# A conv and Fourier-mix kernel on one core: 128-row tiles without overlap, an engine order written by hand, and a second stage on 64-row tiles

## The chip, the core and the metric

The kernel runs on one core of a Trainium2 chip. Its five engines are called as in the profile: PE (matmul, with PEld for the loads of the stationary operand), DVE, ACT, POOL and SP. PE, DVE and ACT reach PSUM; SP and POOL issue the DMAs. The metric is device time in microseconds (us). Three runs of the kernel before gave 261.29, 263.11 and 265.54 us, a median of 263.11 us.

## What is computed

The input x is (8, 3264, 192) in float32: 8 batches, 3264 positions (rows), 192 channels. The first half is a causal convolution of 7 taps along the positions, with one softmax-normalised set of taps for each of 8 heads of 24 channels. The second half is a Fourier layer on the result c: the lowest 64 modes along the positions are mixed by complex 192x192 matrices (`w_r`, `w_i`, one pair a mode), transformed back and added, and a dense layer with a clamp at zero is added on top.

```python
c = conv7_causal(x, softmax(weight))         # per head, along S
X = rfft(c, axis=1)[:, :64]
Yr = Xr @ w_r - Xi @ w_i                     # per mode
Yi = Xr @ w_i + Xi @ w_r
u = c + irfft(Y, n=3264)
out = u + maximum(u @ w_ch, 0)
```

## The kernel before

The positions of a batch are cut into 27 windows of 122 rows. A window is loaded as 128 rows, the 6 rows before it included (`load_win`, L58 to L61), so that one banded 128x128 matrix per head (`cband`) makes 122 rows of convolution in one matmul (`conv_unit`, L214). The loads cast to bf16 on their way into `x_all`; POOL issues them, 3 units of 8 to 10 windows a batch. The convolution's PSUM result goes back into `x_all` by ACT (L226).

`dft` (L268) multiplies each window with a table of cosines and sines (`fst`, made at L143 to L156) and adds 27 windows up into 64 modes for one batch; `xtrans` (L278) turns that round and DVE writes it to `xt` (L286). The mixing loop (L315) then takes 4 modes a turn: 12 matmuls on 32-column tiles of PE (L321) against the mode matrices, which POOL loads through a ring of 6 tiles of 2 modes (L198 to L205). In the same loop the convolved windows are turned by PE into `cT` (`t_unit`, L257, transposes at L264, copies by DVE at L266), since the last stage needs channels on the partitions, and the table is turned into `gst` (`g_part`, L304). The order of the instructions on each engine is made by a scheduler from dependencies and program order; it moves transposes forward into the convolution.

The last stage makes pairs of windows of two batches (`group`, L376). `zp` collects (c + irfft) @ w_ch: one matmul of 384 columns with the table `gst` (L382) and four of 192 columns with `cT` (L386, L387) per window; `yp` gets irfft alone (L388). `zwi`, made by `zwi_pair` (L359), holds the mixed modes multiplied by w_ch and by one. ACT clamps `zp` into `r` (L392), DVE adds `x_all` to `yp` into `t` (L401), and a second add puts `r` on top (L404), on POOL for two groups in three and on DVE for the third. A tile `t` holds 4 windows; `store` (L406) sends it out by SP in 4 DMAs, rows 0 to 111 and rows 112 to 121 of each batch apart. There are 54 groups, three buffers of `t`, and two buffers each of `zp` and `yp`, which fill PSUM.

Of the kernel before, what the change touches and what calls it, by code (L numbers as in the profile page):

```python
# [13 lines left out]
BF16 = mybir.dt.bfloat16  # L14
PSUM = bass.MemoryType.PSUM
# [3 lines left out]
def kernel(  # L19
# [16 lines left out]
    P = 128  # L36
    WIN = 122
    OV = KK - 1
    NWIN = 27
    LASTVALID = S - WIN * (NWIN - 1)  # L40
    PAIRS = NWIN // 2
    NSLOT = 3 * PAIRS + 2
    CTW = NSLOT * WIN + 6
    GW = NWIN * WIN + 6
    MG = 2
    NGRP = MODES // MG
    TWOPI = 2.0 * math.pi
    MAGIC = 12582912.0
    UNITS = ((0, 10), (10, 8), (18, 9))
    USLOTS = ((0, 15), (15, 12), (27, 14))  # L50

    constp = ctx.enter_context(tc.tile_pool(name="const", bufs=1))

    x_all = constp.tile([P, B, NWIN, D], BF16, tag="x_all")

    def load_win(b, c0, n):  # L58
        off = (b * S + WIN * c0 - OV) * D
        src = bass.AP(tensor=x.tensor, offset=x.offset + off, ap=[[D, P], [WIN * D, n], [1, D]])  # L60
        nc.gpsimd.dma_start(out=x_all[:, b, c0:c0 + n, :], in_=src)  # L61

    def load_unit(b, u):
        w0, n = UNITS[u]
        if b == 0 and u == 0:
            nc.gpsimd.dma_start(out=x_all[OV:OV + 112, 0, 0, :], in_=x[0, 0:112, :])
            nc.gpsimd.dma_start(out=x_all[OV + 112:P, 0, 0, :], in_=x[0, 112:WIN, :])
            load_win(0, 1, n - 1)
        elif b == B - 1 and u == 2:
            load_win(b, w0, n - 1)  # L70
# [18 lines left out]

    earlyp = tc.tile_pool(name="early", bufs=1, side="right")
    early_stack = ExitStack()
    ep = early_stack.enter_context(earlyp)
    cband = ep.tile([P, H, P], BF16, tag="cband")
    fst = ep.tile([P, NWIN, 2 * MODES], BF16, tag="fst")
    xt = ep.tile([P, 3, MODES + 1, 2 * B], BF16, tag="xt")

    with tc.tile_pool(name="setup", bufs=1) as sp:
        wraw = sp.tile([P, H, KK], F32, tag="wraw")  # L100
        nc.sync.dma_start(out=wraw[:], in_=bass.AP(tensor=weight.tensor, offset=weight.offset,
                                                   ap=[[0, P], [KK, H], [1, KK]]))
        ones_b = sp.tile([P, P], BF16, tag="ones_b")
        nc.vector.memset(ones_b[:], 1.0)
        maskk = sp.tile([P, KK, P], BF16, tag="maskk")
        for k in range(KK):
            nc.gpsimd.affine_select(out=maskk[:, k, :], in_=ones_b[:], compare_op=ALU.is_equal, fill=0.0,
                                    base=-k, pattern=[[-1, P]], channel_multiplier=1)
        wmax = sp.tile([P, H], F32, tag="wmax")
        nc.vector.reduce_max(out=wmax[:], in_=wraw[:], axis=AX.X)  # L110
        wsub = sp.tile([P, H, KK], F32, tag="wsub")
        nc.vector.tensor_tensor(out=wsub[:], in0=wraw[:],
                                in1=wmax[:, :].unsqueeze(2).to_broadcast([P, H, KK]), op=ALU.subtract)
        wexp = sp.tile([P, H, KK], F32, tag="wexp")
        nc.scalar.activation(out=wexp[:], in_=wsub[:], func=ACT.Exp)
        wsum = sp.tile([P, H], F32, tag="wsum")
        nc.vector.reduce_sum(out=wsum[:], in_=wexp[:], axis=AX.X)
        nc.vector.tensor_scalar(out=wsum[:], in0=wsum[:], scalar1=1e-9, scalar2=None, op0=ALU.add)
        wrec = sp.tile([P, H], F32, tag="wrec")
        nc.vector.reciprocal(out=wrec[:], in_=wsum[:])  # L120
        wsb = sp.tile([P, H, KK], F32, tag="wsb")
        nc.vector.tensor_tensor(out=wsb[:], in0=wexp[:],
                                in1=wrec[:, :].unsqueeze(2).to_broadcast([P, H, KK]), op=ALU.mult)
        for h in range(H):
            nc.vector.tensor_scalar(out=cband[:, h, :], in0=maskk[:, 0, :], scalar1=wsb[:, h, 0:1],
                                    scalar2=None, op0=ALU.mult)
            for k in range(1, KK):
                nc.vector.scalar_tensor_tensor(out=cband[:, h, :], in0=maskk[:, k, :],  # L128
                                               scalar=wsb[:, h, k:k + 1], in1=cband[:, h, :],
                                               op0=ALU.mult, op1=ALU.add)  # L130

        sidx = sp.tile([P, NWIN], F32, tag="sidx")
        nc.gpsimd.iota(sidx[:], pattern=[[WIN, NWIN]], base=0, channel_multiplier=1,
                       allow_small_or_imprecise_dtypes=True)
        midx = sp.tile([P, MODES], F32, tag="midx")
        nc.gpsimd.iota(midx[:], pattern=[[1, MODES]], base=0, channel_multiplier=0,
                       allow_small_or_imprecise_dtypes=True)
        halfpi = sp.tile([P, 1], F32, tag="halfpi")
        nc.vector.memset(halfpi[:], math.pi / 2)  # L140
        kprod = sp.tile([P, NWIN, MODES], F32, tag="kprod")
        turns = sp.tile([P, NWIN, MODES], F32, tag="turns")
        nc.vector.tensor_tensor(out=kprod[:],  # L143
                                in0=sidx[:, :].unsqueeze(2).to_broadcast([P, NWIN, MODES]),
                                in1=midx[:, :].unsqueeze(1).to_broadcast([P, NWIN, MODES]),
                                op=ALU.mult)
        nc.vector.tensor_scalar(out=turns[:], in0=kprod[:], scalar1=1.0 / S, scalar2=MAGIC,
                                op0=ALU.mult, op1=ALU.add)
        nc.vector.tensor_scalar(out=turns[:], in0=turns[:], scalar1=-MAGIC, scalar2=float(S),
                                op0=ALU.add, op1=ALU.mult)  # L150
        nc.vector.tensor_tensor(out=kprod[:], in0=kprod[:], in1=turns[:], op=ALU.subtract)
        nc.vector.tensor_scalar(out=kprod[:], in0=kprod[:], scalar1=-float(S) / 2, scalar2=float(S) / 2,
                                op0=ALU.max, op1=ALU.min)
        nc.scalar.activation(out=fst[:, :, MODES:2 * MODES], in_=kprod[:], func=ACT.Sin, scale=-TWOPI / S)
        nc.scalar.activation(out=turns[:], in_=kprod[:], func=ACT.Abs)
        nc.scalar.activation(out=fst[:, :, 0:MODES], in_=turns[:], func=ACT.Sin, scale=-TWOPI / S,  # L156
                             bias=halfpi[:, 0:1])

    load_unit(0, 2)
    for b in range(1, B):  # L160
        for u in range(3):
            load_unit(b, u)

# [5 lines left out]
    ascale = constp.tile([P, 1], F32, tag="ascale")  # L170
    nc.vector.memset(ascale[:], 2.0 / S)
    nc.vector.memset(ascale[0:1, :], 1.0 / S)
    nc.vector.memset(ascale[64:65, :], 1.0 / S)

    win0 = constp.tile([P, 2 * D], BF16, tag="win0")
    win1 = constp.tile([P, 2 * D], BF16, tag="win1")
    wB0 = constp.tile([P, D], BF16, tag="wB0")
    nc.gpsimd.memset(win0[:, D:2 * D], 0.0)
    nc.gpsimd.memset(win1[:], 0.0)  # L180
# [277 lines left out]
```

## Time and profile before

| what | value |
|---|---|
| runs | 261.29, 263.11, 265.54 us (median 263.11) |
| profiled execution, span from first to last instruction | 264.2 us |
| busy: PE, PEld | 172.3 us (65%), 130.4 us (49%) |
| busy: DVE, ACT, POOL | 154.7 us (59%), 105.9 us (40%), 138.7 us (52%) |
| HBM read, written | 40.31 MB, 20.05 MB |
| mean granted TensorE clock | 0.883 of full speed |

The span counts instructions alone; the page gives no other time of the profiled execution, and the span lies within the three runs. "Busy" is the sum of an engine's instructions; waiting instructions are not in it. The page's slices are 40 equal parts of the span, 6.6 us each. The chain that ended last is followed back from the last instruction, each step to what released it. The trace's GB/s counts the bytes that the DMA engines write, so a cast load of 4-byte numbers into 2-byte ones counts half of what it reads.

### The profile page before, as it was taken

How to read it: one execution, taken by the hardware profiler on the slowest of the kernel's cores; microseconds unless marked ns; L12 is line 12 of the kernel's file. 1: busy time of each engine (PE TensorE's matmuls, PEld its weight loads, DVE VectorE, ACT ScalarE, POOL GpSimd, SP SyncE). 2: the span in 40 equal slices, each digit the busy share in tenths (PEclk: the TensorE clock that was granted, in tenths of full speed). 3: DMA queues.
4: the chain of work that ended last, by engine and by line, in shares of the span. 5: the costliest groups of instructions: out<-in, count | busy, mean ns of one | idle time of the engine just before them, and what ended most of it. 6: DMA issues, size and time to landing. Idle time of an engine off the chain costs nothing.

```text
span 264.2 us, 4507 instructions
## 1 busy us (share of the span) xinstructions
PE 172.3 (65%) x1699; PEld 130.4 (49%) x1699; DVE 154.7 (59%) x264; ACT 105.9 (40%) x140; POOL 138.7 (52%) x154
## 2 busy tenths in 40 slices
PE   0137405508999985978873479887886868877800
PEld 0015204507989973756641157665564547655500
DVE  3997121013344376699971128877865787788730
ACT  2027709205799732211112126453444344445410
POOL 8944435534500017657664016775758497578740
PEclk9999855755999999799996559999999999999965
DMA  5999999999930009999999104876596667877692
GB/s 54 168 192 192 192 192 192 192 192 116 162 59 2 0 2 132 196 175 147 160 169 168 25 0 107 221 204 196 155 258 179 187 169 220 240 219 193 189 254 63
DMA packets 65341, 40.51 MB, mean 153 GB/s; under 512 B 31016, under 2 KB 65320, under 8 KB 65320
## 3 DMA queue, kind: packets, MB, share of 16 engines
q0 software_dynamic: 37600, 20.14, 58.1%
q1 hardware_dynamic: 27720, 20.09, 27.7%
q8 instruction: 13, 0.21, 0.3%
q14 instruction: 8, 0.07, 0.1%
HBM read 40.31 MB, written 20.05 MB: 228 GB/s over the span
## 4 chain that ended last, share of the span: by engine, by line
PE 36%; DMA 27%; DVE 14%; POOL 12%; ACT 4%; issue 3%; SPq 1%; DVEq 0%; POOLq 0%; ACTq 0%
DMA x_all<-in_x_dram 18%; POOL t L404 7%; PE xp L272 7%; DVE t L401 6%; PE cp L220 5%; PE tp L264 5%; DMA wt<-in_moe_w_i_dram 5%; PE zp L382 4%; DMA out_dram<-t 4%; PE zp L386 4%; PE zp L387 4%; DVE cT L266 3%; PE yp L388 3%; ACT r L392 3%; PE yp L321 2%
## 5 line engine op out<-in xcount | busy, mean ns | idle before, releaser
L404 POOL TENSOR_TENSOR t<-t,r 122x768 f32<-122x768 f32 x36 | 69.2, 1944 | 43.2 <-DVE t L401 32.4
L392 ACT ACTIVATE r<-zp 122x768 f32<-122x768 f32 (+1 forms) x54 | 43.1, 809 | 51.3 <-POOL t L404 36.1
L401 DVE TENSOR_TENSOR t<-yp,x_all 122x768 f32<-122x768 f32 (+1 forms) x54 | 50.0, 951 | 21.3 <-PE yp L388 14.6
L226 ACT CAST x_all<-cp 122x960 bf16<-122x960 f32 (+2 forms) x48 | 39.6, 884 | 31.9 <-PE cp L220 21.1
L382 PE MATMUL zp<-zwi,gst 128*128 128x384 bf16 x108 | 35.9, 332 | 18.2 <-ACT r L392 15.4
L386 PE MATMUL zp<-win,cT 128*128 128x192 bf16 x216 | 46.0, 250 | 0.0
L220 PE MATMUL cp<-x_all,cband 128*128 128x240 bf16 (+2 forms) x192 | 31.0, 297 | 20.4 <-DVE cband L128 16.4
L203 POOL DMA_DIRECT2D wt<-in_moe_w_r_dram x32 | 19.5, 611 | 44.2 <-PE yp L321 36.7
L386 PEld LDWEIGHTS <-cT 128*128 128x128 bf16 x216 | 21.4, 99 | 25.6 <-issue 23.8
L220 PEld LDWEIGHTS <-cband 128*128 128x128 bf16 x192 | 20.3, 111 | 26.3 <-DVE cband L128 17.6
L61 POOL DMA_DIRECT2D x_all<-in_x_dram x24 | 23.5, 993 | 18.5 <-DMA x_all<-in_x_dram 18.5
L266 DVE COPY cT<-tp 128x854 bf16<-128x854 bf16 (+2 forms) x48 | 28.4, 609 | 4.2 <-PE tp L264 3.7
L264 PE MATMUL tp<-ident,tl 122*128 122x122 bf16 x112 | 22.1, 228 | 11.1 <-DVE tl L233 10.9
L264 PE MATMUL tp<-ident,x_all 122*128 122x122 bf16 x216 | 26.4, 228 | 3.4 <-DVE cT L266 2.6
L404 DVE TENSOR_TENSOR t<-t,r 122x768 f32<-122x768 f32 (+1 forms) x18 | 25.7, 1430 | 3.3 <-ACT r L392 2.6
L388 PE MATMUL yp<-zwi,gst 128*128 128x384 bf16 x108 | 26.3, 331 | 1.2 <-DVE t L401 1.2
L272 PE MATMUL xp<-x_all,fst 122*128 122x192 bf16 (+1 forms) x216 | 25.4, 265 | 0.8 <-ACT fst L156 0.8
L387 PEld LDWEIGHTS <-cT 128*128 128x128 bf16 x216 | 21.4, 99 | 8.3 <-issue 0.7
L387 PE MATMUL zp<-win,cT 128*128 128x192 bf16 x112 | 24.0, 249 | 0.0
L387 PE MATMUL zp<-wB,cT 128*128 128x192 bf16 x104 | 22.3, 250 | 0.0
L264 PEld LDWEIGHTS <-x_all 122*128 122x128 bf16 x216 | 18.4, 103 | 7.2 <-issue 5.5
L272 PEld LDWEIGHTS <-fst 122*128 122x128 bf16 (+1 forms) x216 | 20.3, 106 | 2.3 <-ACT fst L156 1.2
(83 smaller groups left out, 189.5 us busy)
## 6 DMA issues: line engine op xcount, KB each, us to landing
out_dram<-t SPq DMA_DIRECT2D x48, 336.0 KB
wt<-in_moe_w_r_dram POOLq DMA_DIRECT2D x32, 144.0 KB, 5.0
wt<-in_moe_w_i_dram POOLq DMA_DIRECT2D x32, 144.0 KB, 5.0
x_all<-in_x_dram POOLq DMA_DIRECT2D x8, 432.0 KB, 17.3
x_all<-in_x_dram POOLq DMA_DIRECT2D x9, 384.0 KB, 17.9
x_all<-in_x_dram POOLq DMA_DIRECT2D x7, 480.0 KB, 18.4
out_dram<-t SPq DMA_DIRECT2D x48, 30.0 KB
out_dram<-t SPq DMA_DIRECT2D x8, 168.0 KB
```

The lines of the kernel that those rows point to most:

```text
L220: nc.tensor.matmul(cp[:, j, 0:GRP * n].rearrange("p (w e) -> p w e", w=n), cband[:, h, :], x_all[:, b, w0:w0 + n, GRP * h:GRP * h + GRP], ...
L226: nc.scalar.copy(out=dst, in_=srcv)
L264: nc.tensor.transpose(tp[:, WIN * k:WIN * k + WIN], slot_lhsT(b, u, tl, a + k), ident[0:WIN, 0:WIN])
L266: nc.vector.tensor_copy(out=cT[:, b, WIN * a:WIN * (a + cnt)], in_=tp[:, 0:WIN * cnt])
L272: nc.tensor.matmul(xp[:, 0:D], fst[0:k, c, :], x_all[0:k, b, c, :], start=(c == 0), stop=(c == NWIN - 1))
L382: nc.tensor.matmul(zp[:, k, 0:2 * D], glhs, zwi[:, 0, 2 * q:2 * q + 2, :], start=True, stop=False)
L386: nc.tensor.matmul(o, cT[:, b, WIN * sa:WIN * sa + P], win0[:, 0:D], start=False, stop=False)
L387: nc.tensor.matmul(o, cT[:, b, WIN * sb:WIN * sb + P], wBs[par], start=False, stop=(i == 1))
L388: nc.tensor.matmul(yp[:, k, 0:2 * D], glhs, zwi[:, 1, 2 * q:2 * q + 2, :], start=True, stop=True)
L392: nc.scalar.activation(out=r[0:n, :, :], in_=zp[0:n, :, 0:2 * D], func=ACT.Relu)
L401: nc.vector.tensor_tensor(out=tv, in0=yv, in1=xv, op=ALU.add)
L404: eng.tensor_tensor(out=tk, in0=tk, in1=r[0:n, :, :], op=ALU.add)
```

## The change

The tiles become 25 full ones of 128 rows per batch, without overlap, and a half tile of 64 rows; the half tiles of two batches share the 128 partitions. Two batches are handled as one pair q (`xall[:, slot, i, :]`). The convolution of a tile is now two matmuls per head into one PSUM region, with the band's main block (L228) and, on the tile before, its corner block (L234). A raw tile t sits in slot t+1 and its convolved tile goes to slot t, over the raw tile before it. ACT copies the first four heads out (L242), DVE the last four (L244). The DFT takes both batches of a pair in one matmul of 384 columns (L250). The taps reach the band by 7 predicated copies of 304 elements and four block copies (L167 to L176). Loads come as 24 units of 2 to 5 tiles (mostly 4 or 5), one DMA a batch, plus two for the half tiles.

All transposes now stand in the mixing loop: 48 banks of up to 8 (`g_bank`, `cm_bank`, `ct_bank`), 7 for each two turns of the loop, copied out by DVE twice and ACT once in three. The mode matrices come in a ring of 5 buffers of 4 modes in an area that the setup tables used before and the output tiles use after. The order on each engine is the order of the code (`tc.manual_schedule()`).

The last stage takes 50 units of two tiles of two batches and one unit of half tiles. One PSUM tile of two banks holds both sums: first z, which ACT clamps in place (L459), then y is accumulated on it by PE, and one DVE add with `xall` makes the output (L478). Every contraction of 128 is cut into two of 64 rows; rows 0 to 63 of PE work on one tile of the unit while rows 64 to 127 work on the other, in different banks, and then they change banks (`both`), with a wait on PE's own earlier matmuls in between. POOL adds nothing any more; a unit goes out in two DMAs.

```diff
-    WIN = 122
...
+    UNITS0 = ((0, 2), (2, 4), (6, 5), (11, 5), (16, 5), (21, 5))
+    UNITS = ((0, 5), (5, 5), (10, 4), (14, 4), (18, 4), (22, 4))
...
+    ctx.enter_context(tc.manual_schedule())
...
+    def conv_half(q, t0, n, half):
...
+            nc.tensor.matmul(o, band[:, h, 0:P], xall[:, s0 + 1:s0 + 1 + n, :, dsl], start=(j % 2 == 0), ...)
...
+            nc.tensor.matmul(o[:, k0:n, :, :], band[:, h, P:2 * P], xall[:, s0 + k0:s0 + n, :, dsl], ...)
...
+        if half == 0:
+            nc.scalar.copy(out=dst, in_=srcv)
+        else:
+            nc.vector.tensor_copy(out=dst, in_=srcv)
...
+    for k, u in enumerate(units):
+        conv_half(*u, 0)
+        conv_half(*u, 1)
...
+        if k:
+            dft_unit(*units[k - 1])
...
+    def both(duo, zt, first, which, begin=False, end=False):
...
+        old = held.get(id(zt))
+        if old is not None and old[0] != first and not begin:
+            nop = nc.tensor.nop()
+            for name in old[1]:
+                tc.add_manual_dep(nop.ins, name, ...)
...
+        for k in range(max(len(lists[0]), len(lists[1]))):
+            for row in range(2):
+                lst, bank = lists[row], first ^ row
...
+                mm = nc.tensor.matmul(zt[:, bank, cols], l, r, start=(begin and k == 0), ...)
...
+    def relu(zt):
+        nc.scalar.activation(out=zt[:, :, 0:2 * D], in_=zt[:, :, 0:2 * D], func=ACT.Relu)
...
+        nc.vector.tensor_tensor(out=o[:, :, :], in0=zt[:, :, 0:2 * D], in1=xall[...], op=ALU.add)
...
+    for n in range(N + 2):
+        if n < N:
+            duo, zt = items[n]
+            if n >= ahead:
+                both(duo, zt, 0, "c", begin=True)
+            both(duo, zt, 0, "g")
+        if 0 <= n - 2 < N:
+            both(items[n - 2][0], items[n - 2][1], 1, "y", end=True)
+            finish(n - 2)
+        if n < N:
+            if n >= ahead:
+                both(duo, zt, 1, "c")
+            both(duo, zt, 1, "g")
+            relu(zt)
+        if 0 <= n - 1 < N:
+            both(items[n - 1][0], items[n - 1][1], 0, "y")
-        nc.vector.tensor_tensor(out=tv, in0=yv, in1=xv, op=ALU.add)
-        npool[0] += 1
-        eng = nc.gpsimd if npool[0] % 3 else nc.vector
-        eng.tensor_tensor(out=tk, in0=tk, in1=r[0:n, :, :], op=ALU.add)
```

Two places in PE's order, each before and after, by the names in it. PE in the convolution, before: windows' DFT matmuls (L272, `xp`) stand in between the four matmuls of a convolution half (L220, `cp`).

```order
L272 MATMUL xp<-x_all,fst 128x192
L220 LDWEIGHTS cband
L220 MATMUL cp<-x_all,cband 128x240
L220 LDWEIGHTS cband
L220 MATMUL cp<-x_all,cband 128x240
L220 LDWEIGHTS cband
L220 MATMUL cp<-x_all,cband 128x240
```

The scheduler spreads the 27 DFT matmuls of a batch over the convolution of a later one, three or four between two halves. PE in the convolution, after: the end of a unit's second half (`z_81` is the PSUM tile of that half), the DFT of the unit before (L250), and the next unit's first half, which waits for its load and for ACT to have emptied `z_80`.

```order
L234 MATMUL z_81<-xall,band 128x192
L250 LDWEIGHTS ftab
L250 MATMUL z_82<-xall,ftab 128x384
...
L250 LDWEIGHTS ftab
L250 MATMUL z_82<-xall,ftab 128x384
L228 LDWEIGHTS band [waits DMASW1_49,DMASW0_49]
L228 MATMUL z_80<-xall,band 128x192 [waits Activation_49]
```

A half is now eight matmuls in place of four, and five DFT matmuls of 384 columns stand between two units.

PE in the last stage, before: one window of `zp` and the `yp` of two (`zwi` are the mixed modes, `gst` the table, `cT` the turned windows).

```order
L382 MATMUL zp_2372<-zwi_1770,gst_235 128x384 [waits Activation_49]
L386 LDWEIGHTS cT_240
L386 MATMUL zp_2372<-win0_220,cT_240 128x192
L387 LDWEIGHTS cT_240
L387 MATMUL zp_2372<-wB0_222,cT_240 128x192
L386 LDWEIGHTS cT_240
L386 MATMUL zp_2372<-win0_220,cT_240 128x192
L387 LDWEIGHTS cT_240
L387 MATMUL zp_2372<-wB0_222,cT_240 128x192
```

Six matmuls with `yp`'s make one window of two batches, each over all 128 rows of PE. PE in the last stage, after: the second half of one unit (`z0` to `z3` are the four PSUM tiles; `cm`, `ct` the turned tiles, `ftab` the table, `mixa` the mixed modes). Rows of a pair follow each other, one on each half of PE.

```order
L436 MATMUL z3_83<-mixa_66,ftab_64 128x384 [waits Activation_49]
...
L436 MATMUL z1_81<-wm_68,cm_62 128x192 [waits DVE_49]
...
L436 LDWEIGHTS ftab_64 [waits PE_49]
L436 MATMUL z3_83<-mixa_66,ftab_64 128x384
L436 LDWEIGHTS ftab_64
L436 MATMUL z3_83<-mixa_66,ftab_64 128x384
L436 LDWEIGHTS cm_62 [waits PE_49]
L436 MATMUL z1_81<-wm_68,cm_62 128x192
```

The 12 matmuls of a pair of windows become 20 of half the depth, and two loads of the stationary operand per unit wait for PE itself.

## Rows read from the trace of the kernel before

**Rows 1.** The page: the span.

```profile
span 264.2 us, 4507 instructions
```

**Rows 2.** Windows, whole span: stretch, length, busy us (count) by engine, PEclk, DMA, GB/s.

```profile
0.00:61.00 61.00, 19.25 (x116) 13.53 (x117) 26.14 (x92) 21.09 (x22) 32.81 (x55) 0.79 1.47 174
61.00:98.00 37.00, 35.79 (x408) 32.13 (x407) 17.61 (x18) 27.91 (x34) 6.40 (x11) 0.94 0.37 53
98.00:147.00 49.00, 35.38 (x512) 24.60 (x504) 33.55 (x79) 10.71 (x24) 30.30 (x52) 0.90 1.04 158
147.00:162.00 15.00, 11.03 (x70) 7.00 (x71) 5.15 (x7) 4.65 (x8) 3.62 (x2) 0.63 0.00 0
162.00:257.00 95.00, 70.81 (x608) 53.20 (x606) 72.22 (x71) 41.57 (x53) 65.54 (x34) 0.98 0.75 206
```

**Rows 3.** Waits over the whole span: who waited for whom, total, times, longest.

```profile
POOL wt L203 <- PE yp L321: 36.7, 7, 28.3
ACT r L392 <- POOL t L404: 36.1, 24, 2.5
```

**Rows 4.** Groups of instructions, shapes apart: busy us, mean ns, idle before and releasers.

```profile
L404 POOL TENSOR_TENSOR t<-t,r 122x768 f32<-122x768 f32 x36 | 69.2, 1944 | 43.2 <-DVE t L401 32.4 <-DMA out_dram<-t 7.9 <-ACT r L392 2.7
L401 DVE TENSOR_TENSOR t<-yp,x_all 122x768 f32<-122x768 f32 x52 | 48.1, 951 | 17.9 <-PE yp L388 14.6 <-DMA out_dram<-t 1.6 <-POOL t L404 1.1
L392 ACT ACTIVATE r<-zp 122x768 f32<-122x768 f32 x52 | 41.6, 809 | 48.0 <-POOL t L404 32.7 <-PE zp L387 11.6 <-PE yp L388 2.4
L61 POOL DMA_DIRECT2D x_all<-in_x_dram x24 | 23.5, 993 | 18.5 <-DMA x_all<-in_x_dram 18.5
L386 PEld LDWEIGHTS <-cT 128*128 128x128 bf16 x216 | 21.4, 99 | 25.6 <-issue 23.8
L226 ACT CAST x_all<-cp 122x960 bf16<-122x960 f32 x16 | 15.0, 969 | 12.2 <-PE cp L220 12.0
L286 DVE CAST xt<-tp 128x384 bf16<-128x384 f32 x8 | 14.3, 1793 | 4.2 <-PE tp L284 4.2
L266 DVE COPY cT<-tp 128x976 bf16<-128x976 bf16 x8 | 5.4, 681 | 1.3 <-PE tp L264 1.2
```

**Rows 5.** Windows of steady transfer, columns as in rows 2: x loads, mode matrices, stores.

```profile
14.00:60.00 46.00, 17.21 (x104) 12.56 (x104) 15.79 (x46) 19.33 (x20) 19.34 (x28) 0.73 1.60 192
106.00:116.00 10.00, 9.47 (x125) 6.90 (x115) 7.88 (x19) 2.04 (x5) 6.44 (x12) 0.83 1.19 192
174.00:182.00 8.00, 6.64 (x58) 5.04 (x57) 5.36 (x6) 3.71 (x5) 3.79 (x3) 1.00 0.94 263
240.00:248.00 8.00, 6.82 (x60) 5.26 (x60) 5.61 (x7) 3.24 (x5) 5.23 (x3) 1.00 0.91 246
```

**Rows 6.** Timeline of DVE and ACT in the setup: start, length, instruction.

```profile
5.64 0.26 DVE L122 TENSOR_TENSOR wsb<-wexp,wrec 128x56 f32<-128x56 f32 x1
20.35 1.95 DVE L143 TENSOR_TENSOR kprod<-sidx,midx 128x1728 f32<-128x1728 f32 x1
44.05 1.73 ACT L156 ACTIVATE fst<-turns,halfpi 128x1728 bf16<-128x1728 f32 x1
```

**Rows 7.** The chain that ended last, in order of time: start, us, what.

```profile
97.57 0.73 PE yp L321 x24
...
158.10 0.08 PE zp L386
```

**Rows 8.** Timeline of PE: transposes, five started between the two rows.

```profile
121.08 0.27 PE L264 MATMUL tp<-ident,x_all 122*128 122x122 bf16 x2
...
121.35 0.22 PE L264 MATMUL tp<-ident,tl 122*128 122x122 bf16 x1
```

**Rows 9.** Timeline of PE and SP: end of the mixing, first and last store issued.

```profile
147.48 0.66 PE L321 MATMUL yp<-wt,xt 128*32 128x192 bf16 x10 [1.07 <-DMA wt<-in_moe_w_i_dram]
...
161.41 1.57 SPq L410 DMA_DIRECT2D out_dram<-t  x3
...
257.21 0.26 SPq L426 DMA_DIRECT2D out_dram<-t  x1
```

More of the change, by code (lines that the diff above doesn't have):

```diff
@@ new lines @@
+    NTM = NT + 1
+    kprod = temp(NTM * MODES, F32)
+    turns = temp(NTM * MODES, F32)
+    packed = temp(H * PW, BF16)
+    wraw = temp(H * KK, F32)
+    wsub = temp(H * KK, F32)
+    wexp = temp(H * KK, F32)
+    taps = temp(H * KK, BF16)
+    wmax = temp(H, F32)
+    wsum = temp(H, F32)
+    wrec = temp(H, F32)
+    cidx = temp(PW, F32)
+    masks = temp(KK * PW, U16)
+    sidx = temp(NTM, F32)
+    midx = temp(MODES, F32)
+    Z = [psum.tile([P, 2, 512], F32, tag=f"z{i}", name=f"z{i}") for i in range(4)]
@@ L87 @@
+    nc.scalar.activation(out=tu3, in_=kp3, func=ACT.Abs)
+    nc.scalar.activation(out=ftab[:, :, 0:MODES], in_=tu3, func=ACT.Sin, scale=-TWOPI / S,
+                         bias=halfpi[:, 0:1])
+    for q, t0, n in units[2:5]:
+        load_unit(q, t0, n)
     nc.gpsimd.memset(ident[:], 0.0)
@@ L89 @@
                             base=0, pattern=[[-1, P]], channel_multiplier=1)
[L91 to L162, printed above, removed]
     nc.gpsimd.memset(perm[:], 0.0)
@@ L348 @@
-    while tq:
-        t_unit(*tq.pop(0))
-    early_stack.close()
-    ps1.close()
-    p3 = ctx.enter_context(tc.tile_pool(name="p3", bufs=3, side="right"))
-    zwip = ctx.enter_context(tc.tile_pool(name="zwip", bufs=1, side="right"))
-    zwi = zwip.tile([P, 2, B, D], BF16, tag="zwi")
-    pz = ctx.enter_context(tc.tile_pool(name="pz", bufs=2, space=PSUM))
-    def zwi_pair(q):
-        zp = pz.tile([P, 2, 512], F32, tag="z", name="zwps")
+    nc.gpsimd.memset(xt[:, :, MODES, :], 0.0)
+    for q in range(NQ):
+        nc.gpsimd.memset(ct[0:HALF, q, NF, HALF:P], 0.0)
+        nc.gpsimd.memset(ct[HALF:P, q, NF, 0:HALF], 0.0)
@@ new lines, in load_w, with copy @@
+    def load_w(g):
+        if g < NG:
+            for half, src in ((0, moe_w_r), (1, moe_w_i)):
+                nc.gpsimd.dma_start(out=wts[g % NW][64 * half:64 * half + 64, :, :, :],
+                                    in_=src[4 * g:4 * g + 4, :, :].rearrange("m (p j) e -> p m j e", j=3))
+    for g in range(NW):
+        load_w(g)
+    tbank = [0]
+    ncopy = [0]
+    def copy(out, in_):
+        ncopy[0] += 1
+        if ncopy[0] % 3 == 0:
+            nc.scalar.copy(out=out, in_=in_)
+        else:
+            nc.vector.tensor_copy(out=out, in_=in_)
@@ new lines @@
+    held = {}
+    def both(duo, zt, first, which, begin=False, end=False):
+        lists = (z_pieces(duo[first], 0, which), z_pieces(duo[1 - first], 1, which))
+        old = held.get(id(zt))
+        if old is not None and old[0] != first and not begin:
+            nop = nc.tensor.nop()
+            for name in old[1]:
+                tc.add_manual_dep(nop.ins, name, mybir.DependencyInfo(mybir.DependencyClass.Sync,
+                                                                      mybir.DependencyReason.DATA),
+                                  reason="row tiles take turns on a bank")
+        last = [None, None]
+        for k in range(max(len(lists[0]), len(lists[1]))):
+            for row in range(2):
+                lst, bank = lists[row], first ^ row
+                if k >= len(lst):
+                    continue
+                cols, l, r = lst[k]
+                mm = nc.tensor.matmul(zt[:, bank, cols], l, r, start=(begin and k == 0),
+                                      stop=(end and k == len(lst) - 1), skip_group_check=True)
+                last[row] = mm.ins.name
+        held[id(zt)] = (first, last)
@@ L368, in zwi_pair, with zw_pair @@
+    def zw_pair(q, zt):
+        for i in range(2):
+            b = 2 * q + i
+            nc.tensor.matmul(zt[:, i, 0:2 * D], yet[:, 0, b, :], wm[:], start=True, stop=False)
+            nc.tensor.matmul(zt[:, i, 0:2 * D], yet[:, 1, b, :], w1[:], start=False, stop=True)
+        for i in range(2):
+            dst = zw[:, :, 2 * q + i, :]
+            srcv = zt[:, i, 0:2 * D].rearrange("p (t d) -> p t d", t=2)
             if i == 0:
@@ L406, in store @@
[L406 to L426 removed]
+    seq = [(q, t) for q in range(NQ) for t in range(NF)]
@@ new lines @@
+    items = []
+    zq = 0
+    made = {}
+    for k, duo in enumerate(duos):
+        items.append((duo, Z[k % 4]))
+    for d in range(NG // 2):
+        mix(2 * d)
+        if d == NG // 2 - 1:
+            for n in range(1):
+                for first in range(2):
+                    both(items[n][0], items[n][1], first, "c", begin=(first == 0))
+        mix(2 * d + 1)
+        mix_copy(d)
+        if d < NG // 2 - 1:
+            some(4)
+        else:
+            for first in range(2):
+                both(items[1][0], items[1][1], first, "c", begin=(first == 0))
+        mix_trans(d)
+        if d < NG // 2 - 1:
+            some(3)
+            if d == NG // 2 - 2:
+                some(99)
```

547 lines of the change are left out of this document (307 added, 240 removed).

## The prediction, written before the result was known

> **What bounds the kernel now.** I read the span first: 264.2 us [rows 1], inside the three runs; the sum below is made against it, and the median of 263.11 us is 0.4% less. Then I cut the span into stretches at the points where the kind of work changes [rows 2]. To 61 us the x loads run, at a steady 192 GB/s [rows 5], and PE is busy for a third of the time. From 61 to 98 us it is the other way round: PE is busy for 35.8 of 37 us, and the DMAs carry 53 GB/s, because POOL stands 36.7 us before the loads of mode matrices [rows 3], their ring being full until the mixing begins at 97.57 us [rows 7]. From 98 to 147 us the matrices come at 158 GB/s. Then nothing is moved for 14 us, until the first store is issued at 161.41 us [rows 9]. The stores run at 206 GB/s to 257 us [rows 2], although they reach 246 to 263 in good stretches [rows 5]: the groups come too slowly. The waits say why: ACT waits 36.1 us for POOL's add to free `r` [rows 3], and that add is 1.94 us long, twice DVE's 0.95 [rows 4]. So three things cost time: loading that stops for 31 to 37 us, a gap of 14 us, and 96 us of last stage that the stores alone could do in about 79 (20.05 MB at 255 GB/s, the middle of the two stretches).
>
> **Part one, to the first mixing matmul.** The loads lose the six repeated rows in 128: 26,112 rows for 27,648, so 55 us of loading become 52, and x is there at about 59 us. Twice as many load instructions go through POOL, each with half the rows; even at 0.99 us each [rows 4], not less, 50 would take 50 us, beside the 52 of transfer, so I charge nothing; if that cover is gone, the load ends a few us later, still ahead of PE.
>
> PE sets the end. A matmul of 192 columns takes 0.08 us at the full clock [rows 7], so 0.00042 us a column. The 104 tile pairs (26 by 4) need 16 convolution matmuls of 48 columns and one DFT of 384: 1,152 columns or 0.48 us a pair, 50 us in all. The DFT's columns and the loads of weights are as before, the convolution's double. The transposes, which before stood in this stretch in part, are gone from it. Out of PSUM ACT takes 0.97 us per half of 5 tiles [rows 4] and DVE, at the 1.24 ns an element of its adds, 1.2; a unit of 5 takes PE 2.4 us and each half of PSUM is asked for again after 1.6, so both copies are hidden while PE is the slower.
>
> It starts late: ACT makes the Fourier table before its first copy. DVE has the taps at 5.9 us in the kernel before [rows 6]; the table's first three steps (1.95 us for the first [rows 6], the two others estimated at 1 each) now stand ahead of them, so 10. The 7 predicated copies of 304 elements are not in this trace: between 0.26 us (56 elements, rows 6) and 0.68 us (976 elements, rows 4) each; a line between the two gives 0.37 at this size, and I take 0.45, since three operands are read, so 3.2 us (1.8 to 4.8). Block copies, the table's last two steps (some 3 us together, by the first) and three ACT passes of up to 1.73 us [rows 6] follow: 23 us. From there: 49 us of PE, 2 for a clock that begins at its lower level (granted 0.73 from 14 to 60 us, rows 5), 4 for the `xt` copies (1.79 us each [rows 4], two a pair of batches, in DVE's queue ahead of the next half's copy), and 5 for the last DFT, its turn and two `xt` copies. That makes **84 us** for 97.57. Below, the loads bound it: 59 and some 9 of tail, 68. Above, PE stays as slow as now: 97.6.
>
> **Part two, mixing.** Five of 16 matrix groups (0.59 MB each) are loaded by 75 us, before they are needed. The other eleven follow as buffers come free, at 192 GB/s [rows 5]: 3.07 us each, 34, and 2 for the first issue and the last landing: 36 us, so the last lands at **120** (147.5 now). Every transpose now stands here: 7 banks for two turns, on DVE five copies of 0.7 us [rows 4] and one of the mixed modes, about 4 us, against 6.1 of loading. Hidden; uncovered it would be DVE's 4 us that bounds, which is less. At the pace of the whole stretch before, 158 GB/s, 43 us; with all 11 at 200, 34.
>
> **Part three, the gap.** From the last mixing matmuls to the first store it is 13.9 us now [rows 9]. The chain is the same (copy, turn, two copies, `zwi`, clamp, add), without POOL's add, but the first add waits for three units' matmuls. I take 11 (9 to 14): **131**.
>
> **Part four, the last stage.** A unit of 0.393 MB needs 1.54 us of stores at 255 GB/s. Its two issues on SP cost 1.04 (three took 1.57, rows 9), the clamp 0.81 and the add 0.95 [rows 4]; each has a unit to itself. PE has 20 matmuls. Two halves of rows at once are not in this trace; tiles of 32 columns are: 24 matmuls in 0.73 us, 0.03 each for 0.08 alone [rows 7]. If the halves run side by side, 6 pairs of 192 and 4 of 384 columns are 1.12 us; if one after the other, 2.24. I take the first, since that row shows tiles that run together. Two waits for PE's own matmuls are added. Behind them in PE's queue stands the rest of the unit, and for that ACT and DVE wait. A transpose lasts 0.22 us and the next starts 0.054 later [rows 8]: so some 0.17 us lie behind a matmul's columns, and I charge 0.34, which gives 1.46 for PE (1.12 with the waits covered). The stores are slower by a little; with the two so close I take 1.58, 51 units, **81 us**. With 1 us to the first packet and 1.5 after the last it ends at 214.5; call it 214. The relu and y in one PSUM tile hold it for three units of four; the add of unit n-2 has over a unit's time before its tile is asked for, so I charge nothing.
>
> **A rule against it.** Each cut contraction loads the stationary operand twice. The rows: a load is listed with 99 ns [rows 4], yet five transposes, each with its load of 128 columns, start within 0.27 us [rows 8], so a load takes 54 ns of PE's time or less when hidden; 20 loads are 1.08 us a unit. By that, the trace allows the sum above.
> The Trainium skill ("TensorE: Matmul & The Clock Gate", section "LDWEIGHTS (loading the stationary operand)") has a load cost by its columns, P/1.2 ns, whatever its rows: 107 ns here, as an estimate 2.13 us a unit and 242 us in all. The transposes of this trace start twice as fast, so the trace speaks against it where loads hide; nothing here shows it for halves.
>
> **Rivals.**
> 1. The loads of the two halves go one at a time at their listed 99 ns: 20 are 1.98 us a unit, 101 us; 131 + 2.5 + 101 = 235. For it: the load's row; against it: rows 8. Chance 0.13.
> 2. The halves take turns, the waits covered: 2.24 us a unit, 114 us, 248. Chance 0.08.
> 3. The halves take turns and each wait is bare: 0.17 us and a load of 0.10, twice, make 2.78 us a unit, 142 us, 275. It is slower from 2.64 us a unit on ((268.4 - 133.5) / 51). Chance 0.04; a milder form between 2.43 and 2.64, within 2%, 0.03. For it: no row shows two halves in one matmul's time. Against it: column tiles do it.
> 4. The front isn't PE's but the loads': mixing at 68 us, 198. Chance 0.08: it needs the convolution to start long before 23 us.
> 5. The front stays as slow as now, since ACT, DVE and PE wait for each other's single PSUM halves: mixing at 97.6, 228. Chance 0.09. For it: PE was idle two thirds of the load stretch; against: it was 97% busy from 61 us.
>
> **How the numbers follow.** The forecast, with 0.55, is 214 us. The measurement tells about 2% from no change. The range takes in rivals 1, 2, 4 and 5 from end to end: 197 to 250, which leaves out rival 3, its milder form and what is faster than all bounds. Everything but rival 3 and its milder form is faster by over 2%: 0.93; 0.03 within; 0.04 slower.
>
> **What would show it.** Right: the first mixing matmul near 84 us, PE over 90% busy from 25 us on at the full clock; matrices at some 190 GB/s with a short pause ahead of the mixing; stores near 255 GB/s, 1.6 us a unit; ACT's waits for POOL gone. Wrong: units of 2 us or more with PE full (rival 1 to 3), or stores at 206 GB/s as now while PE waits; DMAs idle long before the mixing (rival 5).

## The result, and the profile after

The changed kernel takes 232.87 us (median of four runs, 231.4 to 235.77) for 262.7 beside it: a ratio of 0.8835, 95% interval 0.8764 to 0.8905. The ratio leaves out runs in a slower state of the clock (here 235.77 us), so it isn't the quotient of the two medians. Forecast were 214 us, 197 to 250. Direction and range hold; the time is 19 us above the forecast, and that is two errors of opposite sign.

The page of the kernel after, its span and its slices (40 of 5.75 us):

```profile
span 230.0 us, 5494 instructions
PE   0010999899799836665866666869989997999960
PEclk9999999999999995589589769599999999999996
DMA  3999999999999004879998860004799997799997
GB/s 43 157 184 188 190 190 191 189 192 189 173 197 206 10 0 64 144 105 153 157 136 133 146 104 0 3 0 126 246 313 286 303 308 236 240 315 310 309 276 250
```

PE is full from slice 5 to 14, then mostly at five to eight tenths for a dozen slices under a clock that comes and goes, then full again. The same by stages, with the columns of [rows 2]:

```profile
0.00:61.00 61.00, 36.68 (x354) 30.74 (x355) 36.99 (x56) 23.18 (x26) 50.16 (x87) 1.00 1.44 171
61.00:87.00 26.00, 20.43 (x220) 16.67 (x218) 15.50 (x13) 7.66 (x10) 3.78 (x7) 0.97 0.65 108
87.00:148.00 61.00, 41.48 (x663) 34.44 (x663) 25.68 (x52) 21.72 (x30) 13.53 (x22) 0.75 0.69 108
148.00:158.00 10.00, 7.49 (x82) 3.77 (x82) 2.90 (x4) 4.55 (x7) 0.00 (x0) 0.88 0.00 0
158.00:230.00 72.00, 61.80 (x992) 40.32 (x988) 49.99 (x53) 39.41 (x51) 0.00 (x0) 0.97 0.91 281
```

Against [rows 2, 7, 9] the front is 10 us shorter (87 for 98), the gap 4, the last stage 31 (72 us from the first store to the end of the span, for 103; stores at 281 GB/s for 206), and the mixing 11 us **longer**: 61 us at 108 GB/s for 50 at 158. Neither PE, DVE nor ACT is full in it. It begins here, in the chain that ended last (start, us, what), where [rows 7] had 97.57:

```profile
87.08 1.15 PE z L366 x21
```

The waits from 87 to 150 us (who for whom, total, times, longest), which answer to [rows 3]:

```profile
POOL arena L297 <- PE z L366: 53.5, 6, 23.0
DVE cm L311 <- PE z L329: 17.3, 14, 2.1
ACT cm L309 <- PE z L329: 12.7, 7, 3.3
PE z L329 <- DVE cm L311: 5.8, 7, 1.0
```

POOL again stands before the loads, but now for mixing matmuls (L366) that come late. DVE and ACT wait for transposes (L329), and PE's transposes wait for copies: they wait for each other. Some 6 us of it in the timeline (start, us, instruction, idle before and releaser):

```profile
107.05 1.07 PE L329 MATMUL z<-ident,xall 128*128 128x128 bf16 x16 [1.00 <-DVE ct L347]
...
107.71 1.29 DVE L311 COPY cm<-z 128x1024 bf16<-128x1024 bf16 x2 [0.71 <-PE z L329]
109.05 0.76 PE L329 MATMUL z<-ident,xall 128*128 128x128 bf16 x8 [0.93 <-DVE cm L311]
...
109.84 1.01 ACT L309 COPY cm<-z 128x1024 bf16<-128x1024 bf16 x1 [3.27 <-PE z L329]
110.02 1.06 PE L329 MATMUL z<-ident,xall 128*128 128x128 bf16 x8
...
111.12 0.69 DVE L311 COPY cm<-z 128x1024 bf16<-128x1024 bf16 x1
111.86 1.87 PE L329 MATMUL z<-ident,xall 128*128 128x128 bf16 x16 [0.78 <-DVE cm L311]
112.92 0.69 DVE L311 COPY cm<-z 128x1024 bf16<-128x1024 bf16 x1 [1.10 <-PE z L329]
```

Eight transposes fill a bank. PE fills two, stands until copies are done, fills one or two more, and stands again: 48 transposes, six banks, in the 6.7 us from 107.05 to 113.73. A round (two turns of the loop: two groups of matrices, seven banks; most expectations below call it a turn) takes 8.4 us on average: the first mixing matmuls of rounds 0 and 7 stand at 87.0 and 146.0 us. The four banks for the transposes are two PSUM tiles of two banks (`Z[0]`, `Z[1]`), filled bank after bank.

The last stage: the first store, a clamp between two adds, and the place where the later mixed modes are multiplied by w_ch (L444 to L452):

```profile
157.79 2.15 SPq L486 DMA_DIRECT2D out_dram<-arena  x4
...
158.04 0.96 DVE L478 TENSOR_TENSOR arena<-z,xall 128x768 f32<-128x768 f32 x1 [0.28 <-PE z L436]
...
158.52 0.80 ACT L459 ACTIVATE z<-z 128x768 f32<-128x768 f32 x1 [0.43 <-PE z L436]
...
159.26 0.96 DVE L478 TENSOR_TENSOR arena<-z,xall 128x768 f32<-128x768 f32 x1 [0.27 <-PE z L436]
...
170.73 0.34 PE L444 MATMUL z<-wm,yet 128*128 128x384 bf16 x1
...
172.30 0.58 ACT L452 ACTIVATE mixa<-z,ascale 128x384 bf16<-128x384 f32 x1 [0.83 <-DVE mixa L450]
172.93 0.34 PE L436 MATMUL z<-wm,cm 64*128 64x192 bf16 x4 [1.38 <-ACT mixa L452]
```

A unit takes 1.22 us (158.04 to 159.26), and every engine waits for PE; twice some 2 us are lost at L452 (unit periods of 3.17 and 3.47 us). In the steadiest stretch the stores go faster than in any of [rows 5] (columns of [rows 2]):

```profile
200.00:220.00 20.00, 20.00 (x344) 13.71 (x339) 15.18 (x17) 12.41 (x17) 0.00 (x0) 1.00 1.01 313
```

### The profile page after: what moved, and what is told of

It is laid out like the page before. It is cut to its first block, busy times and chain, and to the rows that moved or that the text cites. A ratio compares the mean times of both kernels' runs of the same rounds, so it can differ in the third digit from the quotient of the medians.

```text
span 230.0 us, 5494 instructions
## 1 busy us (share of the span) xinstructions
PE 167.9 (73%) x2303; PEld 125.9 (55%) x2303; DVE 131.1 (57%) x177; ACT 96.5 (42%) x123; POOL 67.5 (29%) x115
## 4 chain that ended last, share of the span: by engine, by line
PE 53%; POOL 14%; DVE 12%; DMA 10%; ACT 5%; issue 4%; DVEq 0%; POOLq 0%; ACTq 0%
PE z L436 28%; POOL xall L121 11%; DMA xall<-in_x_dram 10%; PE z L329 7%; PE z L340 4%; DVE cm L311 3%; PE z L366 3%; PE z L228 2%; DVE mixa L271 2%; PE z L234 2%; PE z L250 2%; DVE xall L244 2%; PE z L321 1%; ACT cm L309 1%; DVE ct L311 1%
## 5 line engine op out<-in xcount | busy, mean ns | idle before, releaser
L478 DVE TENSOR_TENSOR arena<-z,xall 128x768 f32<-128x768 f32 x50 | 47.8, 958 | 18.2 <-ACT z L459 10.6
L436 PE MATMUL z<-mixa,ftab 64*128 64x384 bf16 (+1 forms) x432 | 51.1, 317 | 1.7 <-ACT z L459 0.8
L459 ACT ACTIVATE z<-z 128x768 f32<-128x768 f32 x51 | 40.5, 795 | 24.5 <-PE z L436 24.5
L228 PE MATMUL z<-xall,band 128*128 128x192 bf16 (+2 forms) x192 | 26.4, 263 | 25.5 <-ACT band L174 15.1
L244 DVE CAST xall<-z 128x768 bf16<-128x768 f32 (+2 forms) x24 | 25.1, 1047 | 29.6 <-PE z L234 18.7
L121 POOL DMA_DIRECT2D xall<-in_x_dram x48 | 39.5, 840 | 6.6 <-DMA xall<-in_x_dram 5.0
L436 PE MATMUL z<-wm,cm 64*128 64x192 bf16 x408 | 34.9, 250 | 3.1 <-ACT mixa L452 2.7
L242 ACT CAST xall<-z 128x768 bf16<-128x768 f32 (+2 forms) x24 | 20.4, 851 | 34.7 <-PE z L234 24.8
L228 PEld LDWEIGHTS <-band 128*128 128x128 bf16 x192 | 17.9, 102 | 29.1 <-ACT band L174 15.1
L329 PE MATMUL z<-ident,xall 128*128 128x128 bf16 x208 | 19.3, 257 | 10.6 <-DVE cm L311 5.8
L234 PE MATMUL z<-xall,band 128*128 128x192 bf16 (+2 forms) x192 | 26.1, 257 | 0.0
L436 PE MATMUL z<-wt,ct 64*128 64x192 bf16 x208 | 26.0, 247 | 0.0
L329 PEld LDWEIGHTS <-xall 128*128 128x128 bf16 x208 | 16.4, 117 | 13.3 <-issue 12.0
L250 PE MATMUL z<-xall,ftab 128*128 128x384 bf16 x100 | 20.6, 330 | 0.4 <-DVE xall L244 0.4
L234 PEld LDWEIGHTS <-band 128*128 128x128 bf16 x192 | 18.2, 102 | 0.6
```

What stands on the lines that cost most here:

```text
L121: nc.gpsimd.dma_start(out=xall[:, s0:s0 + nf, i, :], in_=src)
L228: nc.tensor.matmul(o, band[:, h, 0:P], xall[:, s0 + 1:s0 + 1 + n, :, dsl], start=(j % 2 == 0), stop=False, skip_group_check=True)
L234: nc.tensor.matmul(o[:, k0:n, :, :], band[:, h, P:2 * P], xall[:, s0 + k0:s0 + n, :, dsl], start=False, stop=not last, skip_group_check=True)
L242: nc.scalar.copy(out=dst, in_=srcv)
L244: nc.vector.tensor_copy(out=dst, in_=srcv)
L250: nc.tensor.matmul(xp, ftab[:, t, :], xall[:, slot(q, t), :, :], start=(t == 0), stop=False, skip_group_check=True)
```

## Experiments: why the mixing takes 61 us

Four causes were open: the two-bank tiles, the clock, the loads, the engines that copy.

**Every bank of the mixing a tile of its own** (pools that are closed before the last stage's tiles are opened):

```diff
-        return ZB[k // 2][:, k % 2, :]
+        return TB[k][:, :].bitcast(BF16)
...
-        yp = Z[2][:, (g // 2) % 2, D * (g % 2):D * (g % 2) + D]
+        yp = YB[(g // 2) % 2][:, D * (g % 2):D * (g % 2) + D]
```

> Edit: in the mixing stage every PSUM bank is a tile of its own (four for the transposes, two each for the mixed modes and their turn), in place of halves of two-bank tiles; nothing else. Theory A (a transpose into the second bank of a tile waits for the copy out of its first bank, so transposes and copies take turns): the mixing stage, 61 us from 87 to 148 in the changed kernel, falls to what the loads of matrices allow, some 40 us, and the kernel to about 210 us. Rival B (PE's low clock makes the transposes themselves the bound): the stage stays above 55 us and PE is over 90% busy in it. Rival C (the loads of matrices bound it): stage and time unchanged, 230 us.

207.68 us (207.09 to 208.53), ratio 0.7879 [0.7814, 0.7945]. Its windows, mixing and last stage:

```profile
87.00:124.00 37.00, 30.47 (x665) 26.18 (x654) 24.25 (x51) 20.93 (x30) 13.53 (x22) 0.94 1.07 178
133.00:205.00 72.00, 61.93 (x994) 40.42 (x992) 49.95 (x53) 39.58 (x51) 0.00 (x0) 0.97 0.91 281
```

The same instructions in 37 us for 61, 5.0 us a round for 8.4; the copies keep DVE as busy as before (24.25 us for 25.68), so the copying engines were not the bound. The last stage is unchanged to 0.1 us of busy PE. From 100 to 120 us the matrices come at 206 GB/s.

**Only the four banks of the transposes**, the mixed modes' tiles left at two banks (the diff is against the run before):

```diff
-    YB = [pr.tile([P, 512], F32, tag=f"yb{i}", name=f"yb{i}") for i in range(2)]
...
+        Z[i] = pr.tile([P, 2, 512], F32, tag=f"w{i}", name=f"w{i}")
```

> The single-bank version with only the four banks of the transposing jobs as tiles of their own; the mixed modes and their turn keep two banks a tile, as in the changed kernel. Theory (the jobs' waits for the other bank of their tile made the mixing long): mixing of 36 to 42 us, 206 to 213 us. Rival (the mixed modes' tiles, of which the next turn's product waits for the copy out of the other bank, had a large share): 216 us or more.

207.46 us (one run): the whole gain lies in those four banks.

**One line, two-bank tiles kept**, but consecutive jobs in different tiles:

```diff
-        return ZB[k // 2][:, k % 2, :]
+        return ZB[k % 2][:, k // 2, :]
```

> The changed kernel (232.9 us) with one line edited: the transposing jobs go to the two two-bank tiles in turn (first bank of one, first bank of the other, second bank of one, ...) and no longer fill both banks of one tile in a row. The tiles stay two banks wide. Theory (a job waits for the copy of the last job in the same tile, so two jobs in a row in one tile stand behind each other): a job now waits for the copy of the job before the last; two jobs overlap, some 0.8 us a job for 1.1, 5.6 to 6.5 us a turn for 8.1, 212 to 223 us. Rival (the jobs wait for each other by something else, by the engines that copy or by the number of banks): 7.5 us a turn or more, 229 to 235 us.

213.16 us (212.6 to 214.9), ratio 0.8094 [0.8056, 0.8131]: 20 us by an index. Its mixing, the window and a piece of the timeline:

```profile
87.00:130.00 43.00, 33.07 (x651) 27.85 (x652) 25.53 (x50) 21.25 (x30) 13.52 (x22) 0.93 0.95 153
```
```profile
103.37 1.38 DVE L311 COPY cm<-z 128x1024 bf16<-128x1024 bf16 x2
103.40 1.32 PE L329 MATMUL z<-ident,xall 128*128 128x128 bf16 x16 [0.39 <-DVE ct L347]
...
105.44 0.77 DVE L311 COPY cm<-z 128x1024 bf16<-128x1024 bf16 x1
105.82 1.05 PE L329 MATMUL z<-ident,xall 128*128 128x128 bf16 x16 [0.42 <-ACT cm L309]
```

PE transposes while DVE copies (103.37 and 103.40), and waits 0.4 us where it waited 0.8 to 1.0. A round is 6.0 us for 8.4. So a job waited for the copy of the job before it because both lay in one tile.

**Work for PE in its waits**, to hold up the clock:

```diff
+        if k % 2 and tbank[0] > 4:
+            for _ in range(10):
+                nc.tensor.matmul(Z[2][:, 0, 3 * P:4 * P], ident[:], wm[:, 0:P], start=True, stop=True, skip_group_check=True)
```

> The changed kernel with ten extra matmuls (128 rows, 128 columns) put into unused columns of a bank ahead of each transposing job that must wait for a copy: they run while TensorE would stand idle, and keep it busy. Theory A (the transposing jobs of the mixing wait in turn for the copies out of the two-bank tiles, whatever the clock): the turns stay at 7 us or more, the mixing still lasts 54 us or more (61.6 before), the time is 224 to 236 us; the granted clock in the mixing rises from some 0.75. Theory B (the mixing is long because the clock falls in its idle stretches): turns of 5.5 us or less, mixing of 44 us or less, 215 us or less. In between: both have a share.

228.7 us (one run). Its windows:

```profile
87.00:100.00 13.00, 10.46 (x132) 9.34 (x125) 3.84 (x6) 3.71 (x5) 4.22 (x7) 0.55 0.64 94
100.00:146.00 46.00, 37.73 (x763) 32.79 (x764) 21.47 (x45) 17.91 (x25) 9.31 (x16) 1.00 0.74 117
```

From 100 us on the clock is whole (0.75 over the stage in the kernel after), and the six rounds behind the first still take 7.9 us, for 8.1 in the kernel after. The low clock was a result of the waits. This one run is some 4 us shorter; what the extra matmuls themselves cost isn't separated from that.

**No matrix loaded in the mixing**:

```diff
-        load_w(g + NW)
```

> Edit: the changed kernel without the loads of matrix groups 5 to 15; the mixing reuses the first five groups (11 of 16 loads are left out). Theory A and rival B: the mixing stage stays within 2 us of its 61 us, since the loads do not hold it. Rival C: it falls to about 45 us or less.

228.42 us (one run). With 1 GB/s on the DMAs the mixing, from its first to its last matmul, lasts 58.6 us for 61.3, 8.2 us a round. That is 0.7 us more than the 2 us of difference expected, under a higher clock (0.82 for 0.75), and far from 45:

```profile
87.00:144.00 57.00, 36.98 (x642) 31.15 (x635) 25.00 (x50) 21.55 (x30) 0.00 (x0) 0.82 0.01 1
```

The loads do not bound the changed kernel. Whether they bound the single-bank version was asked by **three more groups loaded ahead**:

```diff
-    for g in range(NW):
+    for g in range(NW + NE):
...
+    early = [cm[:, 3, 18 * i:18 * i + 18, :].rearrange("p t s -> p (t s)") for i in range(2)]
```

> The single-bank version (207.7 us) with three more groups of mode matrices loaded ahead of the mixing, into the last quarter of the SBUF tiles that the transposes fill later; eight groups instead of eleven are then loaded in the mixing. Theory (in the single-bank version the loads set the mixing: eleven groups of 0.59 MB at 206 GB/s, 2.9 us each): up to three times 2.9 us less; the copies of the transposes, some 4 us a turn, then come next, so 200 to 204 us. Rival (the copies out of PSUM or the turn between engines set the mixing, at some 5 us a turn, already): 206.5 to 208.5 us.

203.75 us (203.12 to 204.09), ratio 0.7747 [0.7712, 0.7781], the fastest of all. The mixing is 34 us, less than half of the 8.7 us at stake came back, and PE is now busy for nine tenths of it:

```profile
87.00:121.00 34.00, 31.11 (x667) 27.24 (x671) 24.39 (x52) 20.61 (x30) 9.83 (x16) 0.92 0.87 141
```

So the loads bounded the single-bank mixing, with PE close behind: the rounds up to 106 us take as long as without the change, and only the last three are shorter (4.1, 4.8 and 3.4 us for 5.3, 5.7 and 5.2).

## Experiments: the last stage and the front

**The last stage over all 128 rows**, on the changed kernel and then on the single-bank version:

```diff
-        r = slice(64 * row, 64 * row + 64)
+        r = slice(0, P)
...
+        lst = z_pieces(duo[first], 0, which)
```

> Edit: the last stage of the changed kernel with contractions of 128 rows in one matmul (the odd channels against weights padded with zeros, as before the change), bank by bank, without the waits for PE's own matmuls. If PE bounds the last stage, as its steady 1.22 us a unit with PE full suggests: 16 matmuls are 3,072 columns, 1.28 us and some 0.1, so 1.38 a unit, 8 us more in all (238). If the stores bound it at 1.22 us a unit (322 GB/s): no change.

The time was inconclusive: 236.72 us median, but four runs from 232.11 to 239.47, with granted clocks from 0.94 down to 0.89 that belong to the mixing. The profile is plain on the unit: 1.31 us for 1.22. (A unit is 12 matmuls there, 8 of 192 columns and 4 of 384, not 16.) So it was asked again where the mixing is quiet:

> The single-bank version (207.7 us) with the last stage's contractions over all 128 rows, one tile after the other, in place of two 64-row halves side by side. By the columns a unit is 8 of 192 and 4 of 384, 1.28 us by 0.08 us for 192, for 1.12 with halves; theory A (halves run side by side and save 0.1 us a unit): units of 1.31 us for 1.22, 207.7 + 51 x 0.09 = 212.3 us (211 to 214). Rival (the halves save nothing: their loads or their waits take it back): 206.5 to 209 us. Rival 2 (the halves were worth half of TensorE's time): 1.9 us or more a unit, 240 us.

210.04 us (209.29 to 211.19), ratio 0.7984 [0.7948, 0.802] beside 0.7879 [0.7814, 0.7945]. The units take 1.31 us, as expected, but only 2.4 of the 4.6 us arrive at the end, below the 211 to 214 of the theory: the last add ends 4.1 us later (203.6 for 199.5), and the span then goes on for 5.0 us, for 6.2. The halves with their waits are worth 0.09 us a unit, and the stores' backlog takes a part of that back.

**The y pieces left out:**

```diff
+        if which == "y":
+            return
```

> The changed kernel with the second product with the mixed modes (the y pieces) left out of the last stage, so TensorE has about 0.32 us a unit less to do. Theory: TensorE sets the last stage's 1.22 us a unit and the stores can go faster than 255 and faster than 313 GB/s: units of 1.04 us (SP's two issues) to 1.1 us, the time 223 to 227 us (232.9 - 51 x 0.12 to 0.18). Rival: the stores are already at their ceiling at 1.22 us a unit (0.393 MB, 322 GB/s): units stay at 1.22, the time at 230 to 235 us.

224.09 us (one run). Units come every 1.06 us, as the theory had it. That is 371 GB/s (0.393 MB in 1.06 us), and the stores take less:

```profile
186.00:205.00 19.00, 17.85 (x294) 11.48 (x296) 16.32 (x18) 14.29 (x19) 0.00 (x0) 1.00 1.00 312
```

At 312 GB/s a unit is 1.26 us of stores; the last add is done at 214.3 us and the span ends at 222.3. PE's 1.22 and the stores' 1.26 lie side by side. The time agrees with the theory in part by luck: the span is 7.7 us shorter, but 3.0 of that are there at the first store (154.8 us for 157.8), ahead of the edit, in a mixing with another clock. The last stage gives 4.7.

**GpSimd's add put back** (on the single-bank version):

```diff
-        nc.vector.tensor_tensor(out=o[:, :, :], in0=zt[:, :, 0:2 * D],
+        nc.vector.tensor_copy(out=o[:, :, :], in_=zt[:, :, 0:2 * D])
+        nc.gpsimd.tensor_tensor(out=o[:, :, :], in0=o[:, :, :],
```

> The single-bank version (207.7 us) with one part of the change undone in the last stage: VectorE copies a unit out of PSUM, and the add of the convolution's result is GpSimd's, as in the kernel before (1.94 us for 128x768). Theory (GpSimd's add had set the pace of the last stage before, and its removal pays for the shorter last stage): units of 1.94 us or a little more, 51 x (1.94 - 1.22) = 37 us more, 243 to 250 us. Rival (the stores or the row halves paid for it): units of 1.22 to 1.4 us, 215 us or less.

219.91 us (one run), between the two. The groups of this run from 125 to 220 us:

```profile
L487 POOL TENSOR_TENSOR arena<-arena,xall 128x768 f32<-128x768 f32 x50 | 80.0, 1659 | 19.8 <-DVE arena L486 19.8
L486 DVE COPY arena<-w 128x768 f32<-128x768 f32 x50 | 47.6, 957 | 26.4 <-PE w L444 10.4 <-ACT w L467 7.6 <-POOL arena L487 4.4
```

POOL starts an add every 1.60 us and is never idle from the first add to the last (its 19.8 us lie ahead of the first), so it sets the pace, as the theory said; but its add, with one operand in bf16, is 1.66 us, not the 1.94 of [rows 4]. Of 49 x 0.38 = 18.6 us, 12.2 arrive, since the two stalls at the late products and the stores' backlog go under.

**Another PSUM tile behind each late product** (on the single-bank version):

```diff
-    items += [(duos[n], Z[n % 4]) for n in range(2, len(duos))]
+    items += [(duos[n], Z[(n + (n > 13) + (n > 26)) % 4]) for n in range(2, len(duos))]
...
-            zw_pair(2 if n == 13 else 3, Z[(n + 1) % 4])
+            zw_pair(2 if n == 13 else 3, Z[(n + 1 + (n > 13)) % 4])
```

> The single-bank version (207.7 us) with the units behind each of the two late products of the mixed modes moved on by one PSUM tile, so that they don't wait for the scaling out of the tile which that product used. Theory: of the two jumps of 2.25 us (unit periods of 3.5 for 1.22) about 0.9 us each stays (0.65 for the product's matmuls, some 0.3 for the add that frees the tile): 205.0 us (204.0 to 206.3). Rival: the add which frees the next tile is as late as the scaling, or the jumps come from the product itself: 207 to 208.5 us.

A miss: 207.31 us (206.91 to 207.96), ratio 0.7872 [0.7844, 0.7899], no change, as the rival had it. One unit of 3.53 us became three of 2.09, 1.85 and 1.85: 2.1 us above 1.22 each, for 2.3. With three tiles in turn, the wait is spread and stays.

**The corner matmuls of the convolution left out:**

```diff
-            nc.tensor.matmul(o[:, k0:n, :, :], band[:, h, P:2 * P], xall[:, s0 + k0:s0 + n, :, dsl],
-                             start=False, stop=not last, skip_group_check=True)
```

> Edit: the convolution of the changed kernel without the corner matmuls of the tile before (left out, so the first rows of each tile lack earlier taps). If PE bounds the front from 23 us on (as the forecast had it): 16 us of matmuls go (104 tile pairs of 8 x 48 columns, 0.16 us each), and the first mixing matmul comes at about 71 us in place of 87, where the x loads begin to bound it. If ACT's and DVE's copies or the loads bound the front: it stays above 82 us.

228.25 us (one run), the first mixing matmul at 80.6 us for 87.1, between the two theories. The front of this run, then the same of the kernel after:

```profile
24.00:80.00 56.00, 45.39 (x368) 32.31 (x366) 36.35 (x33) 21.62 (x27) 31.82 (x46) 0.90 1.34 174
```
```profile
24.00:83.00 59.00, 54.55 (x540) 45.13 (x538) 33.70 (x31) 21.84 (x27) 31.78 (x46) 1.00 1.27 165
```

PE bounds the front of the kernel after. With less to do it idles 10 us and its clock falls to 0.90, so 6.5 of the 16 us go (and the mixing behind it, at 65 us under a lower clock, takes a part of that back); what held it then (its timeline names DVE's casts and `xt` copies) wasn't tried by itself.

## Why the prediction was off by 19 us

By its own steps, forecast against trace: the front +3 us (87.1 for 84; its terms, 23, 49, 2, 4 and 5, add up to 83), the mixing +25 (61 from the first to the last round's matmuls, for 36), the gap -1 (some 9.7 for 11), the last stage -11 (72.2 from the first store to the end, for 83.5). Together 214.5 + 15.5 = 230, the span; the profiled execution took 231.84 us, and the median lies 1 us above it. That the time lies in the range is luck: the range was set by rivals of other causes, and nothing in the prediction made the mixing longer than its loads.

- **The step that failed is "Hidden" in part two.** It set about 4 us of copies in a round against 6.1 of loads, as if four banks were four buffers. The copies' durations on DVE were right (0.69 us each, 25.7 us in 61). But PE, DVE and ACT took turns, because two banks that are filled in a row belong to one tile: 8.4 us a round. With consecutive jobs in different tiles a round is 6.0 us and the time 213.16; with one tile a bank a round is 5.0 us and the mixing 37 us, the forecast's 36 (with loads at 206 GB/s where 192 were forecast). The two-bank tiles stood in the changed kernel's listing; I counted banks.
- **The last stage was mis-sized the other way**, in two terms of part four. Stores: 255 GB/s is the middle of the two stretches in [rows 5], at DMA shares of 0.94 and 0.91, and it was taken for stores of another shape. SP waited only 0.3 and 0.2 us for POOL's adds in these two stretches, so POOL does not explain the rate. With POOL's adds back and the new stores (two DMAs of 128 rows a unit, for pairs of 112 and 10 rows), about the same rate takes less of the DMAs, 0.80 for the 0.91 at 246 GB/s:

```profile
140.00:160.00 20.00, 18.62 (x298) 12.12 (x296) 14.08 (x17) 11.98 (x16) 20.00 (x14) 1.00 0.80 252
```

  At a share of 1.00 the new stores carry 312. What in the shape makes the difference wasn't tried by itself. PE: the two waits for its own matmuls were charged 0.34 us a unit and cost at most 0.10 (1.22 for 1.12). Halves that run side by side were right.
- **Rivals 1 to 3** fall: 20 matmuls with 20 loads in 1.22 us are 61 ns a pair, under the 99 listed. By the rule of the Trainium skill ("TensorE: Matmul & The Clock Gate", "LDWEIGHTS (loading the stationary operand)"), 107 ns a load, a unit would be 2.1 us as an estimate, if its 20 loads came one after the other. Here they don't: the loads hide, for halves too. **Rival 4** falls with the first mixing matmul at 87.1 us. **Rival 5** has the nearest number, 228, but not its cause: the front is 3 us off, and PE is 96% busy in it.
- **The front** was right in kind: behind a first unit of two tiles at 15.1 us, PE's convolution goes on at 23.1 us, after ACT's first copy (23 forecast), and PE is 96% busy from there to 60 us. The 2 us for the clock are in the trace: it has no clock record before 27.4 us, where the column shows 1.00, but four matmuls of 192 columns took 0.64 us at 23.71 and 0.33 at 57.09 (start to start), half the rate, for 4.3 us:

```profile
23.71 0.85 PE L234 MATMUL z<-xall,band 128*128 128x192 bf16 x4
24.35 0.85 PE L228 MATMUL z<-xall,band 128*128 128x192 bf16 x4
...
57.09 0.49 PE L234 MATMUL z<-xall,band 128*128 128x192 bf16 x4
57.42 0.49 PE L228 MATMUL z<-xall,band 128*128 128x192 bf16 x4
```

  The 49 us of PE were too few: a unit of four tile pairs takes 1.97 or 2.13 us for 1.92, and 3.3 where an `xt` pair holds DVE for 3.4 us.
- The gain of the last stage was put on the right cause in part: ACT's wait for POOL is gone, and with POOL's add back the unit is POOL's, but that returns 12 of the 31 us. What gave the other 19 (the stores' new shape, one PSUM tile for both sums) wasn't tried by itself.

## What to carry to other kernels

Count buffers by what the program waits on, not by what the memory offers: two PSUM banks in one tile, filled one after the other, are one buffer to the copies, and an index that alternates tiles gave 20 us of 233, one tile a bank 25. A DMA rate belongs to the transfers it was read from: ask what share of the DMAs they took, and whether the new ones have the same shape. When PE is neither full nor idle and its clock comes and goes, look for engines that take turns first: filling its idle time brought the clock back and some 4 us of 233.

## What the runs showed that was not expected

- Stores of 768-byte rows reach 312 GB/s at a DMA share of 1.00; the best stretch of the kernel before, with DMAs of 112 and 10 rows, had 263 at 0.94.
- Two 64-row halves of PE save 7% of a unit over 128-row matmuls (1.22 for 1.31 us), not half: the columns are 1.12 for 1.28.
- The granted clock fell to 0.53 (87 to 100 us) behind 7 us in which PE had been busy for 2.6, about the lower of its two levels (1.2 and 2.4 GHz); with the waits filled it stayed at 1.00 from 100 us on.
- GpSimd's add of 768 elements a partition is 1.66 us in the run where one operand lies in bf16, and 1.94 where both are f32 [rows 4]. That the type is the cause isn't shown.
